# Attention with Sinkhorn-sorted blocks, then a four-expert MLP: expert 0's token weights loaded as six rows and turned on TensorE

## The chip, the cores and the metric

The kernel runs on one core of a Trainium2 chip. A core has five engines with a queue each: PE (TensorE, matmuls; its weight loads are listed as PEld), DVE (VectorE), ACT (ScalarE), POOL (GpSimd) and SP (SyncE, which here only issues DMAs). Data comes from HBM through 16 DMA engines into SBUF, which has 128 partitions; matmuls write to PSUM. The metric is the device time of one execution in microseconds (us).

## The reference

Batch 4, 8 heads, 768 tokens, head size 64. Sinkhorn normalization makes 8x8 mixing weights per head; they mix the eight blocks of 96 keys and values; each block of queries attends to its mixed block. The result, 3072 tokens of 512, goes through four experts of 512 x 1024 x 512, and the experts' outputs are added with a weight per token and expert.

```python
    for _ in range(5):
        P = P - np.max(P, axis=-1, keepdims=True)
        P = np.exp(P)
        P = P / (np.sum(P, axis=-1, keepdims=True) + 1e-09)
        P = P / (np.sum(P, axis=-2, keepdims=True) + 1e-09)
    k_sorted = np.einsum('bhij,bhjcd->bhicd', P, k_b).reshape(B, H, S, D)
    v_sorted = np.einsum('bhij,bhjcd->bhicd', P, v_b).reshape(B, H, S, D)
...
    p = domain_probs / (domain_probs.sum(-1, keepdims=True) + 1e-09)
    for e in range(E):
        h = np.maximum(x @ w1[e], 0.0)
        out += p[:, e:e + 1] * (h @ w2[e])
```

The change concerns `domain_probs`, 3072 x 4 float32 numbers, of which it touches the rows of the first batch, 768 x 4.

## The kernel before

The order of every engine's work is written out by hand: what stands first in the code comes first in its engine's queue. The stages are: the Sinkhorn steps on 32 partitions (one per batch and head); the attention of batch 0; then the experts for batch 0 while the attention of batch 1 runs between them, and so on, in chunks of 256 tokens; at the end the experts alone.

**The weights of the tokens** are wanted in two forms. For experts 1 to 3 (and for expert 0 later on) they are a row over tokens, copied to all partitions; `spread_weights` makes it through HBM. For expert 0 in batch 0 the second product is made whole for 128 tokens at a time, with the tokens on partitions, so the weight is one number per partition: `p_sb`, 128 x 6, six being the number `R` of token groups of 128 in a batch. `own_weights` computes it in four small DVE operations (L263 to L266) from `p_own`, which holds, on partition p, the four experts' numbers of tokens p, 128 + p, and so on. `second_layer0` uses it (L748) when it moves the product out of PSUM. `p_own` is loaded by SP at L171, with the third DMA of its queue: on the HBM side the pieces are four numbers, 16 bytes, 768 pieces in all. `p_own` lives in a corner of `Tt[2]`, which is unused until later; `room` is a 128 x 4 x 512 float32 tile that first gets the outputs of `second_layer0`.

**The start of each queue.** SP: L77 (the mixing weights), L170 (all of `domain_probs`, in long pieces), L171. POOL: the loads of the first half of the queries (two, L152) and of K (L113), the identity matrix `ident` (two instructions of `make_identity`), the loads of V, K, V (L113) and four of `w1sb[0]` (L183), then masks (L191 to L200), constants, its half of `sn16` (L330), two more loads of queries, two of `w2sb[0]` (L146), whose issue waits for earlier loads to land. PE: `warm(84)`, 84 matmuls on a constant whose result nobody reads; the transposes of the queries `h_q` (L288); `warm(30)`; `r_half(0)`, four matmuls that spread `sn16` over partitions (L342); `mix_half` for K and V, which begins with eight more matmuls on the constant (L507) and then mixes (L521); `r_half(1)`; the scores (L576); and so on. DVE: the Sinkhorn steps (L315 to L321), with the steps of `spread_weights` between them, its half of `sn16` (L330), then `build_PI0` (L353), which turns `ps_R`, the result of `r_half(0)`, into the mixing matrix that L521 reads.

**PSUM.** Two pools of two buffers each, `psM` and `psA`, every buffer of two banks. A tile of `psM` takes the buffer of the last but one tile before it and waits until that one's readers are through. The first tiles of `psM` are, in turn: `warm(84)`'s, `warm(30)`'s, `ps_R`, the first `mix_half`'s. Where the pools are closed for the last stage (`last_banks`, L1104), the tiles that follow lie over the old buffers.

Of the kernel before, what the change touches and what calls it, by code (L numbers as in the profile page):

```python
# [10 lines left out]
F32 = mybir.dt.float32  # L11
# [7 lines left out]
def kernel(  # L19
# [11 lines left out]
    nc = tc.nc  # L31

    B, H, S, D = q.shape
# [4 lines left out]
    E = moe_w1.shape[0]  # L38
    FF = moe_w1.shape[2]
    P = 128  # L40
# [3 lines left out]
    R = BLK // CP  # L44
# [27 lines left out]
    def psm(shape, dtype, name):  # L72
        return psM.tile(shape, dtype, tag="ps", name=name)
# [27 lines left out]
    room = const.tile([P, 4, Dm], F32, name="room")  # L101
# [5 lines left out]
    def load_natural(b, nm, qd, parts=1, between=None):  # L107
        src = {"k": k, "v": v}[nm]
        t = arena[:, ds(("k", "v").index(nm) * 2 * NW + qd * NW, NW)].rearrange("p (h r d) -> p h r d", h=4, r=R)
        natural[(b, nm, qd)] = t  # L110
        n = 4 // parts
        for m in range(0, 4, n):
            nc.gpsimd.dma_start(  # L113
                t[:, ds(m, n)].rearrange("p h r d -> p h (r d)"),
                src[b, ds(4 * qd + m, n)].rearrange("h (p r) d -> p h (r d)", r=R),
            )
            if m == 0 and between:
                between()
# [31 lines left out]
    def load_half_queries(hf):  # L150
        for qd in range(2):
            nc.gpsimd.dma_start(  # L152
                q0[ds(64 * qd, 64), hf].rearrange("p h r d -> p h (r d)"), half_queries(qd, hf)
            )
# [7 lines left out]
    def p_part(at, n):  # L162
        return Tt[2].rearrange("p a f x -> p (a f x)")[:, ds(2 * at, 2 * n)].bitcast(F32)
# [4 lines left out]
    p_own = p_part(2 * E * NT + NT, R * E).rearrange("p (t e) -> p t e", e=E)  # L168
    own_den = p_part(2 * E * NT + NT + R * E, R).rearrange("p (t o) -> p t o", o=1)
    nc.sync.dma_start(p_in, moe_domain_probs.rearrange("(p t) e -> p t e", t=NT))  # L170
    nc.sync.dma_start(p_own, moe_domain_probs[0:S].rearrange("(t p) e -> p t e", p=P))  # L171
    load_half_queries(0)
    load_natural(0, "k", 0)


    ident = const.tile([P, P], F16, name="ident")
    make_identity(nc, ident)
    load_natural(0, "v", 0)
    load_natural(0, "k", 1)
    load_natural(0, "v", 1)  # L180
# [91 lines left out]
    def warm(n):  # L272
        ps = psM.tile([P, 4, P], F32, tag="ps", name=f"ps_w_{state['n']}")
        state["n"] += 1
        for m in range(n):
            nc.tensor.matmul(ps[:, m % 4, :], dummy, dummy, start=True, stop=True)
# [3 lines left out]
    def h_q(qd, hf, copy, ps=None):  # L280

        if ps is None:
            ps = psa([P, 2, R, 64], F16, f"ps_q_{qd}_{hf}")
        rows = ds(64 * qd, 64)
        for sg in range(2):
            for r in range(R):
                for hh in range(2):
                    nc.tensor.transpose(  # L288
                        ps[ds(D * hh, D), sg, r, :], q0[rows, hf, 2 * sg + hh, r, :], ident[rows, rows]
                    )  # L290
        if copy:
            copy(qT0[qd][:, :, hf], ps[:])
# [16 lines left out]
    for it in range(5):  # L309
        nc.scalar.activation(sn[:], sn[:], AF.Exp, bias=0.0, scale=1.0)  # L310
        if it == 4:
            for qd in range(2):
                h_q(qd, 0, nc.scalar.copy)
            warm(30)
        nc.vector.tensor_reduce(srow[:], sn[:], AX.X, ALU.add)  # L315
        nc.vector.reciprocal(srow[:], srow[:])
        nc.vector.tensor_tensor(sn[:], sn[:], srow[:].broadcast_to([GH, NB, NB]), ALU.mult)
        nc.vector.tensor_reduce(scol[:], sn[:].rearrange("p i j -> p j i"), AX.X, ALU.add)
        nc.vector.reciprocal(scol[:], scol[:])
        if it < 4:  # L320
            nc.vector.tensor_tensor(  # L321
                sn[:], sn[:],
                scol[:].rearrange("p j o -> p o j").broadcast_to([GH, NB, NB]),
                ALU.mult,
            )
            if it:
                next(p_steps)

    for a, eng in enumerate((nc.vector, nc.gpsimd)):
# [4 lines left out]
            ALU.mult,  # L334
        )

    ps_R = psM.tile([P, 2, 512], F32, tag="ps", name="ps_R")
    Rv = ps_R[:, :, 0:HB * GH].rearrange("p a (i g) -> p a i g", g=GH)

# [1238 lines left out]
```

## Time and profile before

| | us |
|---|---|
| median of 3 runs | 358.63 |
| lowest, highest of them | 358.15, 358.74 |
| the profiled execution | 358.21 |
| its span, from the first to the last instruction | 356.3 |
| PE idle in 0 to 11.60, of 11.60 | 2.30 |
| PE idle in 11.60 to 20, of 8.40 | 0.60 |
| PE idle in 20 to 320, of 300 | 0.14 |
| PE idle in 320 to 356.3 | 2.86 |

Lines of the profile are read so: start and length in us, engine, line of the kernel, operation, what it writes and reads, the shapes, the count; in brackets the idle time of the engine before it, and who ended it. In the groups by line, the numbers behind the bar are busy time and mean ns of one. In tables by stretch, each engine's busy time is followed by the granted PE clock, the busy share of the DMA engines (over 1 where several packets of one engine are under way) and GB/s.

The loads of the first 60 us stand one behind another: the page has the DMA engines busy for at least nine tenths of nearly every slice up to 140 us, at some 200 GB/s.

```profile
DMA  8999999999999999743995410005200014100021
GB/s 104 203 205 230 212 209 194 207 195 167 195 180 166 195 116 203 138 88 44 180 205 91 107 74 0 2 1 136 78 26 3 2 37 141 62 0 2 0 75 46
```

### The profile page before, as it was taken

The numbers are of one execution on the slowest core, as the hardware profiler recorded it, in microseconds if no ns is written. First come the engines' busy times: TensorE is split into PE (matmuls) and PEld (weight loads), VectorE is DVE, ScalarE is ACT, GpSimd is POOL, SyncE is SP. The second block draws the span as 40 slices with busy tenths as digits, with TensorE's granted clock in tenths as the row PEclk, the third lists the DMA queues.
The fourth block names the chain that finished last, engine by engine and source line by source line (L and its number), as shares of the span: only waits on it lengthen the run. The fifth ranks groups of instructions, "written<-read, shape, count | busy, mean of one in ns | idle before, by whom it ended". The sixth has DMA issues, their size and how long they took to land.

```text
span 356.3 us, 9511 instructions
## 1 busy us (share of the span) xinstructions
PE 350.4 (98%) x3948; PEld 305.5 (86%) x3948; DVE 277.5 (78%) x555; ACT 170.1 (48%) x302; POOL 137.6 (39%) x154
## 2 busy tenths in 40 slices
PE   8899999999999999999999999999999999999996
PEld 8686857888888888988899888888888888888886
DVE  5766787779798687778879988896678886588963
ACT  2653330452425445368847259830288611598301
POOL 8766112466022420000626318840068800188400
PEclk9999999999999999999999999999999999999999
DMA  8999999999999999743995410005200014100021
GB/s 104 203 205 230 212 209 194 207 195 167 195 180 166 195 116 203 138 88 44 180 205 91 107 74 0 2 1 136 78 26 3 2 37 141 62 0 2 0 75 46
DMA packets 74762, 40.26 MB, mean 113 GB/s; under 512 B 41568, under 2 KB 70496, under 8 KB 74720
## 3 DMA queue, kind: packets, MB, share of 16 engines
q0 software_dynamic: 38720, 19.93, 43.2%
q1 hardware_dynamic: 35856, 19.67, 27.2%
q8 instruction: 31, 0.51, 0.6%
q14 instruction: 11, 0.09, 0.1%
q10 hardware_dynamic: 144, 0.07, 0.1%
HBM read 41.88 MB, written 6.34 MB: 135 GB/s over the span
## 4 chain that ended last, share of the span: by engine, by line
PE 95%; DVE 3%; issue 0%; DMA 0%; ACT 0%; DVEq 0%
PE ps_h L815 18%; PE ps_Q L1296 18%; PE ps_p L799 12%; PE ps_X L1153 10%; PE ps_Z L1153 7%; PE ps_Q L1153 7%; PE ps_Z L1296 6%; PE ps_h L704 3%; PE ps_o L741 3%; PE ps_p L860 3%; PE ps_a L479 2%; PE ps_s L444 2%; PE ps_k L425 1%; PE ps_v L391 1%; PE ps_mv L521 1%; PE ps_a L593 0%
## 5 line engine op out<-in xcount | busy, mean ns | idle before, releaser
L815 PE MATMUL ps_h<-xT,w 128*128 128x256 f16 x576 | 67.5, 273 | 0.0
L815 PEld LDWEIGHTS <-w 128*128 128x128 f16 x576 | 55.2, 98 | 7.3
L821 DVE SCALAR_TENSOR_TENSOR Hb<-ps_h,pb 128x1024 f16<-128x1024 f32 x34 | 41.5, 1223 | 17.8 <-PE ps_h L815 17.6
L1153 PEld LDWEIGHTS <-w 128*128 128x128 f16 x480 | 43.6, 98 | 4.7
L1166 POOL TENSOR_TENSOR arena<-tmp,pb 128x512 f16<-128x512 f32 x12 | 15.2, 1276 | 65.7 <-PE ps_Z L1153 49.8
L1296 PEld LDWEIGHTS <-Hb 128*128 128x128 f16 x320 | 31.1, 98 | 3.5
L1165 ACT ACTIVATE tmp<-tmp 128x512 f32<-128x512 f32 x46 | 29.0, 632 | 3.9 <-DVE tmp L1203 3.9
L1296 PEld LDWEIGHTS <-Sb 128*128 128x128 f16 x304 | 28.2, 98 | 3.0
L1153 PEld LDWEIGHTS <-arena 128*128 128x128 f16 x312 | 27.7, 98 | 2.8
L451 ACT ACTIVATE ET<-ps_s 96x768 f16<-96x768 f32 x24 | 18.1, 802 | 25.2 <-PE ps_s L444 25.0
L434 ACT CAST kT<-ps_k 64x384 f16<-64x384 f32 x48 | 22.7, 473 | 13.3 <-PE ps_k L425 12.3
L126 POOL DMA_DIRECT2D arena<-in_q_dram x24 | 19.9, 842 | 20.8 <-DMA q_ring<-arena 17.7
L1153 PE MATMUL ps_X<-ET,arena 128*128 128x256 f16 x168 | 25.2, 272 | 0.0
L1296 PE MATMUL ps_Q<-w,Hb 128*128 128x256 f16 x192 | 24.6, 273 | 0.0
L799 PEld LDWEIGHTS <-Hb 128*128 128x128 f16 x232 | 21.9, 98 | 3.0
L1159 DVE SCALAR_TENSOR_TENSOR Hb<-ps_X,pb 128x512 f16<-128x512 f32 x27 | 18.7, 692 | 7.0 <-PE ps_X L1153 7.0
L1173 ACT COPY ps_X<-ps_Z 128x512 f32<-128x512 f32 x27 | 15.4, 571 | 17.8 <-PE ps_Z L1153 17.8
L1153 PE MATMUL ps_Z<-xT,w 128*128 128x256 f16 (+1 forms) x176 | 22.5, 258 | 0.0
L785 DVE TENSOR_TENSOR Sb<-Hb 128x512 f16<-128x512 f16 x33 | 20.6, 646 | 0.0
L1180 ACT COPY tmp<-ps_X 128x512 f32<-128x512 f32 x26 | 15.2, 586 | 9.2 <-PE ps_X L1153 6.6
L1159 DVE SCALAR_TENSOR_TENSOR Hb<-ps_Z,pb 128x512 f16<-128x512 f32 x27 | 18.4, 683 | 1.3 <-PE ps_Z L1153 1.3
L1203 DVE TENSOR_TENSOR tmp<-ps_Q,tmp 128x512 f32<-128x512 f32 x26 | 17.7, 683 | 0.8 <-PE ps_Q L1153 0.8
(270 smaller groups left out, 744.3 us busy)
## 6 DMA issues: line engine op xcount, KB each, us to landing
w<-in_moe_w_dram POOLq DMA_DIRECT2D x4, 1024.0 KB, 27.2
w<-in_moe_w_dram POOLq DMA_DIRECT2D x6, 512.0 KB, 19.7
arena<-in_k_dram POOLq DMA_DIRECT2D x7, 384.0 KB, 7.6
arena<-in_v_dram POOLq DMA_DIRECT2D x7, 384.0 KB, 8.1
vs<-arena SPq DMA_DIRECT2D x36, 66.0 KB, 5.3
arena<-in_q_dram POOLq DMA_DIRECT2D x24, 96.0 KB, 7.5
out_dram<-ob SPq DMA_DIRECT2D x9, 256.0 KB, 2.0
pb<-p_dram SPq DMA_DIRECT2D x4, 512.0 KB, 5.8
```

What stands on the lines that cost most here:

```text
L126: nc.gpsimd.dma_start(t[:, h // 2, :, h % 2, :], q[b, h].rearrange("(t p) d -> p t d", p=P))
L434: nc.scalar.copy(kT[ds(D * hh, D), r], pk[ds(D * r, D), hh].rearrange("p a (i c) -> p a i c", c=CP),)
L451: nc.scalar.activation(ETs[2 * (pr % 2) + hh][:, 0:S].rearrange("c (a x) -> c a x", a=2), pss[hh][0:BLK, :, 0:HS], AF.Exp, bias=0.0, scale ...
L785: tt(sm[0], blk(0, 1), blk(1, 1), ALU.add)
L799: nc.tensor.matmul(ps, lhs(e, f), Ts[e][rhs][:, f, :], start=(first and e == es[0] and f == 0), stop=(done and e == es[-1] and f == KH - 1 ...
L815: nc.tensor.matmul(ps[:, f, :], w1sb[e][:, kc, ds((4 * g + f) * P, P)], xT[:, kc, ds(2 * c * P, 2 * P)], start=(kc == 0), stop=(kc == NKC ...
L821: nc.vector.scalar_tensor_tensor(out=Hb[:, homes.get(e, e), ds(4 * g, 4), :], in0=ps[:], scalar=0.0, op0=ALU.max, in1=weights(e).broadcast ...
L1153: nc.tensor.matmul(dst[:, ds(f * cols, cols)], a[lhs][:, k, ds((f0 + f) * P, P)], t[rhs][:, k, :], start=(first and f == 0 and k == 0), st ...
L1159: nc.vector.scalar_tensor_tensor(out=home(i, j), in0=src.rearrange("p (f x) -> p f x", f=m), scalar=0.0, op0=ALU.max, in1=weight(j).broadc ...
L1165: nc.scalar.activation(src, src, AF.Relu, bias=0.0, scale=1.0)
L1203: tt(t12, Q, u2, ALU.add)
L1296: nc.tensor.matmul(ps, lhs(e, f), Ts[e][rhs][:, f, part], start=(first and e == 0 and f == 0), stop=(e == E - 1 and f == KH - 1), skip_gro ...
```

## The change

The load at L171 now fills six partitions of `room` instead of 128 of `p_own`: row t holds the 512 numbers of tokens 128 t to 128 t + 127, one piece of 2 KB. POOL copies the 6 x 6 corner of the identity as float32 into `room`, right behind `make_identity`. The second warming loop makes 14 matmuls instead of 30. Behind the Sinkhorn steps, between the two halves of `sn16` and `ps_R` in the code, PE multiplies, for each expert e, the six rows' numbers of that expert (128 weight columns, a step of four numbers) with the identity into `ps_own`, a new tile of `psM`; DVE copies the 24 numbers per partition to `p_own`, where `own_weights` reads them as before. Both operands are float32.

```diff
-    nc.sync.dma_start(p_own, moe_domain_probs[0:S].rearrange("(t p) e -> p t e", p=P))
+    own_rows = room[0:R, 1, :].rearrange("t (p e) -> t p e", e=E)
+    nc.sync.dma_start(own_rows, moe_domain_probs[0:S].rearrange("(t p) e -> t p e", p=P))
     load_half_queries(0)
     load_natural(0, "k", 0)
...
     ident = const.tile([P, P], F16, name="ident")
     make_identity(nc, ident)
+    ident32 = room[0:R, 0, 0:R]
+    nc.gpsimd.tensor_copy(ident32, ident[0:R, 0:R])
     load_natural(0, "v", 0)
...
             for qd in range(2):
                 h_q(qd, 0, nc.scalar.copy)
-            warm(30)
+            warm(14)
...
+    ps_own = psm([P, E, R], F32, "ps_own")
+    for e in range(E):
+        nc.tensor.matmul(ps_own[:, e, :], own_rows[:, :, e], ident32, start=True, stop=True)
+    nc.vector.tensor_copy(p_own.rearrange("p t e -> p e t"), ps_own[:])
     ps_R = psM.tile([P, 2, 512], F32, tag="ps", name="ps_R")
```

In the queues: PE has the four products behind the 14 warming matmuls and ahead of L342; DVE has the copy between L330 and L353; POOL has its copy ahead of the loads of V, K, V and of `w1sb[0]`; SP and ACT have the same instructions in the same order. In `psM`, `ps_own` follows `warm(14)`'s tile, `ps_R` takes that one's buffer, and the first `mix_half`'s tile takes the buffer of `ps_own`, so that L507 waits for DVE's copy where it waited for `warm(30)`. From there on every tile of `psM` lies in the other buffer than before.

## The prediction

> **What bounds the kernel now.** I read the page first: the busy times, the slices, the chain of work that ended last.
>
> ```profile
> span 356.3 us, 9511 instructions
> ...
> PE 350.4 (98%) x3948; PEld 305.5 (86%) x3948; DVE 277.5 (78%) x555; ACT 170.1 (48%) x302; POOL 137.6 (39%) x154
> ...
> PE   8899999999999999999999999999999999999996
> ...
> PE 95%; DVE 3%; issue 0%; DMA 0%; ACT 0%; DVEq 0%
> ```
>
> PE is busy for 350.4 of 356.3 us. The 5.9 us in which it isn't lie almost wholly in the first two slices and the last one. So from about 20 us on, whatever the start has lost or gained goes one to one into the end, and nothing that the change touches after that (the four small operations that make the weights, at 21 us on DVE) is on PE. The question is only what happens to the first 20 us. There I read the time lines of PE and DVE, in order of time.
>
> ```profile
> 7.73 0.85 PE L288 MATMUL ps_q<-ident,T 64*64 64x64 f16 x48
> 8.51 1.85 PE L276 MATMUL ps_w<-Hb 128*128 128x128 f16 x30
> 11.60 0.26 PE L342 MATMUL ps_R<-ident,sn 32*128 32x32 f16 x4 [1.24 <-DVE sn L330]
> 11.79 0.62 PE L507 MATMUL ps_mk<-Hb 128*128 128x128 f16 x8
> ```
>
> ```profile
> 10.86 0.68 DVE L330 TENSOR_TENSOR sn<-sn,scol 32x512 f16<-32x512 f32 x1
> 11.97 0.75 DVE L353 TENSOR_TENSOR Sb<-maskk,ps_R 128x256 f16<-128x256 f16 x2 [0.43 <-PE ps_R L342]
> ```
>
> Up to 11.54 us DVE runs the Sinkhorn steps without a break, and PE only fills time: 30 warming matmuls to 10.36 us, then 1.24 us of idling until DVE's L330 releases L342. DVE then idles 0.43 us until L342 is through. The change puts its PE work into the first of these gaps and its DVE copy into the second.
>
> The third place is the loads. The weight-load rows of PE around 16 us, and the issue of the last V load (issued at 5.62 us):
>
> ```profile
> 15.86 0.20 PEld L576 LDWEIGHTS <-kT 64*128 64x128 f16 x8
> 16.14 0.46 PEld L521 LDWEIGHTS <-arena 128*64 128x64 f16 x24
> ...
> ```
>
> ```profile
> arena<-in_v_dram POOLq DMA_DIRECT2D x1, 384.0 KB, 10.5
> ```
>
> L576's weight loads end at 16.06, L521's begin at 16.14, and the V rows that they read land at 5.62 + 10.5 = 16.1. So here PE waited for a DMA, for some 0.08 us; it is too short for the list of waits. All other early loads have room: the K rows before them (issued 4.88, 9.3 us to landing: 14.2) are used at 14.40, the last part of w1 (issued 8.43, 13.0 us: 21.4) at 21.84.
>
> **The change, part by part.** The sum is made against the profiled execution: 358.21 us, of which the span is 356.3. The median of the runs is 358.63, 0.42 more.
>
> *Sixteen warming matmuls go.* Thirty take 1.85 us, 0.056 each after the pipeline's 0.2, so 0.90 us less of PE: the fourteen are through issuing at 8.51 + 14 x 0.056 = 9.3 us instead of 10.2. They write nothing that is read: off the path. Their cover is the idle stretch; what they could cost by missing is the clock (second rival).
>
> *Four float32 matmuls come, at 9.3 us.* Their inputs are long there: the six rows are issued at 1.66, as the old load was (landed 3.9 us later), and POOL's copy of the identity is done before 5 us. No row is float32. Low end: L342, the same kind of small product (128 weight columns, 32 moving), four in 0.26 us. High end: the slowest weight load and the slowest matmul of L276 (151 and 314 ns), not overlapped and doubled for operands twice as wide: 4 x 0.93 = 3.7 us. Nearest is L342, so I take it doubled for the width, 0.5 us: end at 9.8. They must be done by 11.54, so up to 2.2 us (0.55 each) costs nothing; at the high end they end at 13.0, 1.4 us late.
>
> [...]
>
> *DVE's copy out of PSUM*, 24 values per partition: low 0.16 us, high 0.31 (DVE's L263 and L252 on float32 rows of 6 and 96 values); I take 0.20, the mean of L606, which reads float32 from PSUM. It starts behind L330 at 11.57 and ends at 11.77, at 11.88 at the high end: both before 11.97, when L353 starts, which waits for L342 anyway. Queued behind it on DVE is L353, and PE's L521 waits for that. Cost 0.
>
> *PSUM ring.* The new tile is one more in a ring of two, so the warming matmuls of L507 now wait for DVE's copy. Copy end plus the 0.06 us that L342 took after L330 is 11.83, against 11.79 before: 0.04 us later (0.15 at the high end). But L521 starts at 12.45, 0.06 behind the first half of L353 (11.97 + 0.75/2 = 12.35 or a little later), and eight matmuls at 0.056 from 11.83 are issued by 12.28. Cost 0. All later tiles of the ring swap places, with the same predecessors in time.
>
> *POOL's copy of 6x6* stands ahead of three K and V loads, four w1 loads, the masks and POOL's half of L330. Low 0.13 us (POOL's L210), high 0.37 (L191, 128x64); I take 0.2. The loads: each is issued more than 7 us before it lands, behind a backlog, below. POOL's L330 ends at 12.46 + 0.2, or 12.83; PE's second L342, which waits for it, starts at 13.32. Cost 0; without that cover it would be the 0.2.
>
> *The load.* The DMA view of 2.70 to 5.05 us, by queue (packets, MB, share of 16 engines):
>
> ```profile
> q0 software_dynamic: 346, 0.25, 73.5%
> q1 hardware_dynamic: 784, 0.01, 26.9%
> ```
>
> The 768 pieces of 16 bytes are in q1: 26.9% of 2.35 us is 0.63 us of every engine. Six packets of 2 KB take their place. What follows in the backlog (q, k, v, w1 in turn; the rows below are two stretches of it, with DMA share and GB/s last) can land up to 0.63 us sooner; from below, 0 if the engines weren't the limit. Either way PE gains at 16.14 only what it waited, 0 to 0.08 us, since from 16.06 on it is held by its own order and by DVE. I take half, 0.04, but in a run that lies above the profiled one more of it may be this wait.
>
> ```profile
> 2.75:3.75 1.00, 1.00 (x12) 1.00 (x11) 0.86 (x5) 0.00 (x0) 0.98 (x2) 1.00 0.38 30
> 3.75:5.00 1.25, 1.25 (x15) 1.25 (x13) 0.82 (x5) 0.26 (x1) 1.19 (x3) 1.00 1.54 183
> ```
>
> Sum: 0 + 0 + 0 + 0 + 0 - 0.04: 358.17 against 358.21; for the median of runs about 358.5.
>
> **The rivals.**
>
> *Float32 matmuls too long (slower).* Place: PE between 9.3 and 11.54; it decides from 0.55 us for each on. Then L342, L353 and all behind them shift. For it: nothing in the trace shows their price, and the high end of the rows is beyond the point. Against: the small products here pipeline at 65 ns each. Price 0 to 1.4 us; with a typical 1.2: 359.8.
>
> *The clock of PE falls (slower).* From 1.06 to 5.04 us the time line has 38 matmuls in 3.98 us, from 5.04 to 7.60 it has 49 in 2.56: the same matmul, at half the rate first. If the thinner stretch from 9.3 to 11.6 brought that state back for another 4 us, PE, busy for 3.71 of the 4.00 us from 11.60, would lose up to half of that: 1.85 us, 360.5. Against: the 1.24 us of idling did not do it, and with the new matmuls at 0.5 us the idling is 1.8 us.
>
> *The loads gain more (faster).* The first row above moves 30 GB/s while the 16-byte pieces are at their thickest, the second 183. If the pieces cause that, 1.00 x (1 - 30/183) = 0.84 us come on top of the 0.63. What PE can take of it is the wait at 16.14 in an ordinary run: 0.08 and, if all that lies between the median and the profiled execution is this wait, 0.42 more, and a little behind it where w1's parts follow closely; 0.5 to 0.9 us, 357.9. Against: the second row runs at the full rate with the pieces still in it, and the other waits have room.
>
> *It doesn't do what it says.* The second row speaks for it: nothing lands sooner, and nothing is lost: 358.6.
>
> **How the numbers follow.** Forecast 0.42 (358.5, own range 358.1 to 358.9); no effect on the loads 0.24; long matmuls 0.13; the clock 0.07; loads gain more 0.14. 0.2% is 0.7 us, about what a measurement of this kernel can tell from no change. Of the last case I count two thirds beyond it (0.09), and 0.03 of the first two for scatter: faster 0.12. Of the long matmuls three quarters (0.10), the clock wholly (0.07) and 0.03 of scatter: slower 0.20. Same: 0.68. The range reaches down to 357.8, through most of the faster case, and up to 359.8, the typical long matmul; it leaves out the clock and the tails, under 0.2.
>
> **What would show it.** In the profile after: fourteen L276 rows and then four products on the new tile that end before 11.54; the DVE copy between L330 and L353, L353 still at 11.97; L507 about 0.04 later, L521's first start the same; POOL's half of L330 0.2 us later; V's last landing before 16.06 and the 0.08 us of PE's loads gone; PE's 40.00 of 40.00 later on unchanged. I am wrong if L342 starts after 11.60, if the matmuls behind it take twice their time, or if the end differs by more than what has been gained or lost at 20 us.

## The result, and the profile after

The changed kernel takes 359.9 us (median of 11 runs, 358.86 to 362.4) against 358.43 before on the same chip (11 runs, 358.04 to 359.75): 1.0039 times the time before, 95% interval 1.002 to 1.0058. It is slower, by 1.5 us in the medians. The profiled execution takes 360.24 us, its span is 358.3, 2.0 longer than before.

The page of the changed kernel: busy times, PE's row of slices, the granted clock, the chain that ended last.

```profile
span 358.3 us, 9499 instructions
...
PE 354.0 (99%) x3940; PEld 309.3 (86%) x3940; DVE 277.7 (78%) x556; ACT 170.5 (48%) x302; POOL 137.8 (38%) x155
...
PE   8999999999999999999999999999999999999996
...
PEclk9789999999999999999999999999999999999999
...
PE 99%; DVE 0%; issue 0%
```

PE is busy for 3.6 us more than before, although 16 warming matmuls of 0.056 us are gone. What is new is in the row of the granted clock, the 7 and 8 of the second and third slices; before, this row is 9 throughout:

```profile
PEclk9999999999999999999999999999999999999999
```

Cut into stretches (us, busy time and count of PE, PEld, DVE, ACT and POOL, granted clock, DMA share, GB/s), the changed kernel has:

```profile
7.10:13.93 6.83, 6.65 (x156) 6.28 (x155) 4.95 (x20) 1.97 (x5) 6.58 (x21) 1.00 1.27 190
13.93:20.76 6.83, 6.83 (x129) 5.77 (x124) 3.64 (x8) 4.94 (x9) 4.52 (x6) 0.50 1.26 204
20.76:60.00 39.24, 39.10 (x515) 28.49 (x513) 29.79 (x54) 14.49 (x20) 14.19 (x19) 1.00 1.28 211
```

From 13.93 to 20.76 us PE's clock is granted at half, and in no other stretch behind 7.10 us. Before, the clock is 1.00 from 5.04 us to the last matmuls. The two ends lie 6.83 us apart, twice the 3.41 us for which the clock is at half in one of the kernels below (v1, from 12.54 to 15.95). All 11 timed runs of the changed kernel have a mean clock of 0.986 to 0.995; of 117 runs of the kernel before, over all the comparisons below, three do.

The time lines of PE and of DVE after, in the form of those shown of before:

```profile
8.71 0.85 PE L291 MATMUL ps_q<-ident,T 64*64 64x64 f16 x48
9.49 0.96 PE L279 MATMUL ps_w<-Hb 128*128 128x128 f16 x14
10.38 2.02 PE L342 MATMUL ps_own<-room 6*128 6x6 f32 x8
12.27 0.25 PE L349 MATMUL ps_R<-ident,sn 32*128 32x32 f16 x4
12.70 0.61 PE L514 MATMUL ps_mk<-Hb 128*128 128x128 f16 x8 [0.18 <-DVE T L343]
```

```profile
11.06 0.68 DVE L333 TENSOR_TENSOR sn<-sn,scol 32x512 f16<-32x512 f32 x1
...
12.44 0.20 DVE L343 COPY T<-ps_own 128x24 f32<-128x24 f32 x1 [0.70 <-PE ps_own L342]
12.63 0.75 DVE L360 TENSOR_TENSOR Sb<-maskk,ps_R 128x256 f16<-128x256 f16 x2
```

The four products are eight matmuls, each with a weight load, and take 2.02 us. DVE waits 0.70 us for them, and L360 (L353 before) starts at 12.63 instead of 11.97. The copy L343 is now what L514 waits for.

The loads did land earlier: the K and V rows of the first halves are issued at 2.71, 4.30, 5.06 and 5.80 us and land at about 9.5, 11.5, 13.7 and 15.4 (issue plus 6.8, 7.2, 8.6 and 9.6 us), the last one 0.7 us earlier than the 16.1 of before. (With the six rows alone, y2 below, that row lands at 16.4, so the gain isn't even sure to be theirs.) At half the clock PE comes to them later anyway.

### The profile page after: what moved, and what is told of

Its sections match the earlier page's. It is cut to its first block, busy times and chain, and to the rows that moved or that the text cites. A ratio compares the mean times of both kernels' runs of the same rounds, so it can differ in the third digit from the quotient of the medians.

```text
span 358.3 us, 9499 instructions
## 1 busy us (share of the span) xinstructions
PE 354.0 (99%) x3940; PEld 309.3 (86%) x3940; DVE 277.7 (78%) x556; ACT 170.5 (48%) x302; POOL 137.8 (38%) x155
## 4 chain that ended last, share of the span: by engine, by line
PE 99%; DVE 0%; issue 0%
PE ps_h L822 18%; PE ps_Q L1303 18%; PE ps_p L806 12%; PE ps_X L1160 10%; PE ps_Z L1160 7%; PE ps_Q L1160 7%; PE ps_Z L1303 6%; PE ps_o L748 3%; PE ps_h L711 3%; PE ps_p L867 3%; PE ps_w L279 2%; PE ps_a L486 2%; PE ps_s L451 2%; PE ps_k L432 1%; PE ps_v L398 1%; PE ps_s L583 1%
## 5 line engine op out<-in xcount | busy, mean ns | idle before, releaser
L1303 PEld LDWEIGHTS <-Sb 128*128 128x128 f16 x304 | 28.2, 98 | 3.0
L1180 ACT COPY ps_X<-ps_Z 128x512 f32<-128x512 f32 x27 | 15.4, 571 | 17.7 <-PE ps_Z L1160 17.7
```

What stands on the lines that cost most here:

```text
L1303: nc.tensor.matmul(ps, lhs(e, f), Ts[e][rhs][:, f, part], start=(first and e == 0 and f == 0), stop=(e == E - 1 and f == KH - 1), skip_gro ...
```

## The experiments

Times are medians; the ratio is to the kernel before on the same chip, whose medians there are 358.32 to 358.37 us (358.43 beside the changed kernel). It is an estimate from all runs and need not be the quotient of the medians. "Clock low" counts the runs whose mean granted clock is below 0.998. Line numbers shift by a few from kernel to kernel.

| kernel | first, second warming | products | us (range) | ratio, 95% interval | clock low |
|---|---|---|---|---|---|
| after | 84, 14 | float32 | 359.9 (358.86 to 362.4) | 1.0039 (1.002 to 1.0058) | 11 of 11 |
| x1 | 84, 30 | float32 | 359.33 (358.82 to 361.71) | 1.0048 (1.0027 to 1.0069) | 2 of 7 |
| x2 | 84, 14 | none | 359.75 (359.0 to 360.41) | 1.0039 (1.0027 to 1.0051) | 5 of 5 |
| x3 | 84, 30 | none | 358.97 (358.1 to 361.67) | 1.0033 (1.0013 to 1.0053) | 2 of 12 |
| x4 | 84, 30 | float16 | 360.0 (358.11 to 361.8) | 1.0038 (1.002 to 1.0055) | 5 of 12 |
| y1 | 84, 30 | none | 358.1 (357.88 to 360.1) | 1.0002 (0.9989 to 1.0016) | 1 of 12 |
| y2 | 84, 30 | none | 358.41 (358.07 to 359.31) | 0.9995 (0.9985 to 1.0006) | 0 of 12 |
| y3 | 84, 14 | none | 360.42 (358.83 to 362.5) | 1.005 (1.0033 to 1.0067) | 12 of 12 |
| y4 | 84, 44 | none | 360.13 (359.85 to 360.6) | 1.0047 (1.0033 to 1.0061) | 0 of 5 |
| z1 | 76, 30 | float32 | 359.58 (358.05 to 361.42) | 1.0026 (1.0008 to 1.0044) | 7 of 12 |
| z2 | 68, 30 | none | 359.71 (358.12 to 360.99) | 1.0024 (1.0008 to 1.0041) | 11 of 12 |
| z3 | 84, 22 | none | 358.04 (358.02 to 358.67) | 0.9992 (0.9981 to 1.0004) | 0 of 11 |
| z4 | 92, 30 | none | 359.16 (358.37 to 360.69) | 1.0027 (1.001 to 1.0043) | 0 of 12 |
| v1 | 84, 14 + 16 thin | none | 359.8 (358.61 to 361.27) | 1.0033 (1.0018 to 1.0048) | 11 of 12 |
| v2 | 84, 15 wide | none | 358.23 (358.04 to 359.01) | 0.9992 (0.9981 to 1.0003) | 0 of 12 |
| v3 | 84, 15 wide | float32 | 358.71 (358.13 to 360.37) | 1.0007 (0.9992 to 1.0023) | 1 of 12 |

**First four: warming against products.** All are the changed kernel with an edit.

x1, the warming matmuls back:

```diff
-            warm(14)
+            warm(30)
```

> The changed kernel with the second warming loop at 30 matmuls again; the float32 products stay behind it. Three theories of the 1.5 us. Clock: PE's rate is halved for one or more stretches of 3.4 us, because the float32 products (8 records, 0.23 us apart, six columns each) keep PE occupied and let almost nothing pass; then the products still lie in front of L342 and the rate falls in most runs, mean clock 0.995 or below, and 359 to 361 us. Late: the products end too late, and 16 warming matmuls more push them 0.9 us further back: clock 1.000 and 0.5 to 0.9 us over the changed kernel's undisturbed time, 359.0 to 359.5. Warming: the 16 missing matmuls alone starved the clock: clock 1.000 in all runs.

x2, no products (a constant stands where they wrote), 14 warming matmuls; x3, the same with `warm(30)`:

```diff
-    ps_own = psm([P, E, R], F32, "ps_own")
-    for e in range(E):
-        nc.tensor.matmul(ps_own[:, e, :], own_rows[:, :, e], ident32, start=True, stop=True)
-    nc.vector.tensor_copy(p_own.rearrange("p t e -> p e t"), ps_own[:])
+    nc.vector.memset(p_own, 0.25)
```

> The four products and the copy out of PSUM are left out, a constant is written to p_own instead (expert 0's weights in batch 0 are wrong numbers); six-row load, POOL's copy and warm(14) stay. Clock by what PE streams: without the products the stretch is just as thin, so the rate still falls, mean clock 0.990 to 0.995, 359 to 360. Products themselves (their lateness, or a clock that only they disturb): clock 1.000, 358.2 to 358.5.

> As the one without products, with 30 warming matmuls: what is left of the change is the load of six rows and POOL's 6x6 copy. All theories: clock 1.000, and the time of the kernel before less what the earlier loads bring, 0 to 0.5 us: 358.0 to 358.4. Slower than 358.8 would mean that the load or POOL's copy has a price.

x4, the rows cast to float16 on POOL, the products in float16, and `warm(30)`:

```diff
+    own16 = room[0:R, 0, 0:2 * P].bitcast(F16).rearrange("t (e p) -> t e p", e=E)
+    nc.gpsimd.tensor_copy(own16, own_rows.rearrange("t p e -> t e p"))
...
+        nc.tensor.matmul(ps_own[:, e, :], own16[:, e, :], ident[0:R, 0:R], start=True, stop=True)
```

> The products in float16 (POOL casts the six rows, 6x512, in place of its 6x6 copy; the weights are rounded to float16), 30 warming matmuls. If the float32 form is what costs, four records of under 0.1 us each stand in place of 1.9 us of products: clock 1.000 and 358.1 to 358.5. If four more products and a copy cost in any form: 358.8 or more.

Without the products but with 14 warming matmuls the clock fell in every run and the time stayed at that of the changed kernel: the products are not what the loss hangs on. With 30 the clock held in five of seven runs (x1) and ten of twelve (x3), yet the medians did not come back wholly: 359.33 and 358.97. In float16 the products take four matmuls in 0.25 us, half of what the prediction took for float32:

```profile
9.68 0.25 PE L342 MATMUL ps_own<-ident,room 6*128 6x6 f16 x4
```

That kernel's seven runs with the clock held lie between 358.11 and 360.3, and in five of twelve it fell. It also changes more than the type: POOL's cast of the rows takes 1.14 us where the 6x6 copy took 0.18, and the first V load behind it is issued at 5.14 us instead of 4.30. This group told the clock from the products, but left x1, x3 and x4 unexplained: two runs of x3 stand at 361.18 and 361.67, one of x1 at 360.75 and two of x4 at 360.03 and 360.3, at a clock of 0.999 or 1.0. No profile of such a run was taken, and nothing later settled them.

**Second four: each part alone.** y1, y2 and y3 are the kernel before with one part of the change. y1, POOL's copy only:

```diff
+    ident32 = room[0:R, 0, 0:R]
+    nc.gpsimd.tensor_copy(ident32, ident[0:R, 0:R])
```

> The kernel before with one addition: POOL's 6x6 float32 copy behind the identity. With it (changed kernel and three variants) DVE's first L321 took 0.28 to 0.34 us in place of 0.21, and the Sinkhorn steps ended 0.14 to 0.2 us later. Theory POOL: that copy alone moves L330 from 10.86 to 11.0 us, so 0.14 us in an undisturbed run (358.4 to 358.6), and PE, idle longer, loses its clock in some of the runs (359 to 361.7), as in the variant without products and with 30 warming matmuls. Theory load: the six-row load disturbs, POOL's copy does not: 358.0 to 358.7 as before, no run above 359.

y2, the six-row load only (with the constant of x2 for `p_own`):

```diff
-    nc.sync.dma_start(p_own, moe_domain_probs[0:S].rearrange("(t p) e -> p t e", p=P))
+    own_rows = room[0:R, 1, :].rearrange("t (p e) -> t p e", e=E)
+    nc.sync.dma_start(own_rows, moe_domain_probs[0:S].rearrange("(t p) e -> t p e", p=P))
...
+    nc.vector.memset(p_own, 0.25)
```

> The kernel before with the six-row load alone (no 6x6 copy on POOL, no products, 30 warming matmuls; p_own gets a constant, so expert 0's weights in batch 0 are wrong numbers). Theory POOL: nothing is prolonged, V's last rows land at 15.4 to 15.8 us instead of 16.1: 358.0 to 358.4, no run above 359. Theory load: spread as in the variant with POOL's copy, median near 359, some runs at 361.

y3, 14 warming matmuls only:

```diff
-            warm(30)
+            warm(14)
```

> The kernel before with 14 warming matmuls in place of 30 and nothing else. Theory clock by what PE streams: PE is thin from 9.3 to 11.6 us whatever else is there: the rate falls in all or most runs, mean clock 0.995 or lower, 359 to 360.4 us. If the 16 matmuls don't matter for the clock and only the products or POOL's copy do: 358.0 to 358.7, clock 1.000.

y4, x3 with `warm(44)` in place of `warm(30)`:

> Six-row load and POOL's copy, no products (a constant in p_own), and 44 warming matmuls: PE streams to about 11 us, with 14 x 0.056 = 0.8 us less idling. Theory clock: no run loses the rate, 358.2 to 358.6, the 0.14 us of POOL's copy remaining; in an execution whose rate rises late they end behind the Sinkhorn steps and cost up to 0.5 us. If the slow runs of the variant with 30 have another cause (loads, DVE), they stay: some at 360 to 361.7.

POOL's copy alone (y1) and the load alone (y2) do nothing that can be measured. Both together, as x3 has them, gave 1.0033 on another chip; that difference stays open. Taking the sixteen warming matmuls from the kernel before, and nothing else, gives the whole loss, and the lower clock in 12 of 12 runs. Its stretches:

```profile
6.50:13.30 6.80, 5.13 (x150) 4.71 (x150) 5.19 (x21) 1.91 (x5) 6.58 (x20) 1.00 1.24 178
13.40:20.10 6.70, 6.70 (x124) 5.64 (x119) 3.64 (x8) 4.80 (x9) 4.04 (x6) 0.50 1.26 205
```

The same half clock, with nothing new on PE. The runs fall into steps by their mean clock: two at 0.995, 358.83 and 358.84; those at 0.99 from 359.64 to 359.78; at 0.986 from 360.36 to 360.72 (one more, 362.5 at 0.99, fits no step). One step lower costs 0.8 to 0.9 us; as an estimate, 0.004 to 0.005 of a span of some 358 us is 2.9 to 3.6 us more at half rate. How many steps it is differs between executions of this one kernel.

y4 is listed at a clock of 1.0 in every run and still takes 360.13. (Its profile and x1's hold no clock rows, so the listed 1.0 is no proof by itself; but its matmuls run at the full rate: the 24 of L525 at 14.59 us take 0.57 us, as in the kernel before, against 0.85 in the changed kernel at half the clock.) Its list of waits in 18 to 33 us (engine, what waited, for what: total, times, longest) holds two stops that no shown event ends:

```profile
PE ps_a L597 <- issue: 0.8, 1, 0.8
PE ps_w L552 <- issue: 0.8, 1, 0.8
```

So a second way of losing time came up, with more instructions on PE, not fewer. z4 was made for it.

**Third four: where, how many, and the count.** z1 is the changed kernel with `warm(76)` and `warm(30)`; the other three are the kernel before with `warm(68)` (z2) or `warm(92)` (z4) in the first group, or `warm(22)` in the second (z3).

```diff
-    warm(84)
+    warm(68)
```

> The changed kernel with the 30 warming matmuls ahead of the float32 products and the first warming cut from 84 to 76, so that PE issues as many instructions ahead of L349 as in the kernel before (a float32 product takes two weight loads and two matmuls, four products as much as eight warming matmuls). Theory (the 16 matmuls that are missing right ahead of the products cost the clock; the float32 products themselves only delay the start by up to 0.5 us, most of which is taken up by 68 us; the 1.0 us of the run with 30 and 84 was mostly a stall of PE that moved with the count of instructions): every run at a granted clock of 1.0, 358.3 to 358.9 us. Rival (the products themselves cost the microsecond, wherever PE's instructions fall): 359.2 to 359.5 again. Rival (the products' 2 us of thin work lower the clock also here): a clock of 0.99 in most runs, 359.7 to 360.4.

> The kernel before with the first warming cut from 84 to 68 and nothing else: 16 warming matmuls fewer, as in the run with 14 instead of 30, but taken from the first group, and the same count of PE's instructions as there. Theory (it is the work right ahead of L342 that keeps the clock): all or nearly all runs at 1.0 and 358.1 to 358.6 us. Rival (it is the number of warming matmuls, or of instructions, wherever they stand): a clock of 0.995 to 0.986 and 359.6 to 360.6 us as in that run.

> The kernel before with 22 instead of 30 warming matmuls in the second group. Theory (a bound that is passed or not: with 30 the clock held in nearly every run, with 14 in none): runs of two kinds, at a clock of 1.0 and about 358.2 us, and at 0.99 and 359.7 to 360.0 us. Rival (each missing warming matmul costs its share): all runs near 359.3 us at a clock between.

> The kernel before with the first warming raised from 84 to 92 and nothing else: 16 instructions of PE more ahead of L342 (a load and a matmul each), as many as the changed kernel with 30 warming matmuls has; nothing on the critical path, and the clock kept. Theory (a stall of PE that waits for nothing the profile shows moves with the count of instructions): clock 1.0 and 358.8 to 359.3 us, with an issue wait of 0.7 to 1 us in PE's rows somewhere behind 18 us. Rival (the count does nothing, and the microsecond in the run with 30 and 84 came from the products): 358.1 to 358.5 us.

Three of these theories fell. Taking the sixteen from the first group lowers the clock as well (z2, 11 of 12 runs): it is not the place right ahead of L342 that counts. With 22 all eleven runs kept it (z3): neither two kinds of runs nor a share for each missing matmul, but a bound between 14 and 22. And in z1, with the 30 right ahead of the products but eight fewer in the first group, the clock fell in 7 of 12, though the profiled run kept it; its five runs that kept it stand at 358.05 to 359.29, median 358.41 against 358.35 before. z4's theory came true: with eight warming matmuls more, off the path, it lost 0.8 us in the medians at a full clock in all runs. Its profile, of its quickest run (358.37), has a shorter stop of the same kind, and one of 0.2 us at L704:

```profile
13.63 0.29 PE L521 MATMUL ps_mv<-Sb,arena 128*64 128x64 f16 x7 [0.39 <-issue]
```

That more instructions on PE can cost time is shown by z4's median, 359.16 against 358.35. What PE waits for in these stops no view of this case shows, and no run tests it.

The profiles now allowed a table. Cut from the rise of its clock into stretches of 3.41 us, half of the 6.83 above, each execution has one stretch ahead of the kernel's end in which PE does the least while the clock is full. Its work is counted as rows x weight columns x streamed columns of the matmuls that start in it, in units of a warming matmul (128 x 128 x 128; at 0.056 us 61 of them fill a stretch; by L741 of before, where 24 matmuls of 512 columns take 5.18 us, 63, of which 20.5 and 21.6 are 0.32 and 0.34).

| execution | stretch from | matmuls | work | clock after it |
|---|---|---|---|---|
| z2 | 8.19 | 17 | 17.0 | 0.5 |
| after | 10.51 | 63 | 19.3 | 0.5 |
| y3 | 9.95 | 58 | 20.5 | 0.5 |
| x2 | 10.28 | 64 | 20.5 | 0.5 |
| x4 | 10.57 | 64 | 20.5 | 0.5 |
| z4 | 12.95 | 66 | 21.6 | 1.0 |
| z3 | 8.82 | 27 | 23.2 | 1.0 |
| y1 | 10.57 | 72 | 23.3 | 1.0 |
| z1 | 8.28 | 32 | 24.0 | 1.0 |

The work orders them; the number of matmuls doesn't (64 and a fall, 27 and none), nor does busy time (PE is busy for 95% of that stretch in the changed kernel, 50% in z3). Idle time doesn't either; the same row in y3's stretch and in z3's, with the idle time at its end:

```profile
L342 PE MATMUL ps_R<-ident,sn 32*128 32x32 f16 x4 | 0.3, 174 | 1.6 <-DVE sn L330 1.6
L342 PE MATMUL ps_R<-ident,sn 32*128 32x32 f16 x4 | 0.3, 174 | 1.7 <-DVE sn L330 1.7
```

y3 idles for 1.6 us and loses the clock, z3 for 1.7 and keeps it. Of the other profiles with clock rows, before, x3 and y2 do least with 30 to 32 and keep it. That was a fit to profiles already seen, so it had to foretell something.

**Last three: is it the work?** v1 and v2 are the kernel before, v3 the changed kernel; `warm` gets a second loop: v1 has 14 matmuls as they were and 16 `thin` ones, v2 and v3 have 15 `wide` ones and none of the old.

```diff
+        for m in range(thin):
+            nc.tensor.matmul(ps[:, m % 4, :], dummy[0:8], dummy[0:8], start=True, stop=True)
...
+        for m in range(wide):
+            nc.tensor.matmul(
+                ps[:, ds(2 * (m % 2), 2), :], dummy,
+                dummy.rearrange("p (o x) -> p o x", o=1).broadcast_to([P, 2, P]), start=True, stop=True,
+            )
```

> The kernel before with 14 warming matmuls of 128 rows and then 16 of 8 rows in place of 30 of 128: as many instructions and as much busy time of PE as before, but of the work of the array (rows by columns by streamed columns) that of 14 and one more. Theory (the clock goes by the work of the array in a stretch of 3.4 us: in the profiles so far it fell behind stretches with at most 0.32 of the full work and held behind all with 0.34 and more): it falls in nearly all runs as with 14, to 0.995 to 0.986, 358.8 to 360.6 us with a median near 359.8. Rival (it goes by busy time or by the number of matmuls): a clock of 1.0 and 358.0 to 358.7 us as before.

> The kernel before with 15 warming matmuls of 256 streamed columns in place of 30 of 128 in the second group: the same work of the array in half the instructions. Theory (work of the array): a clock of 1.0 in nearly all runs, and 358.0 to 358.7 us. Rival (the number of matmuls): a lower clock and 359.6 to 360.6 us as with 14.

> The changed kernel with 15 warming matmuls of 256 streamed columns in place of its 14 of 128: the work of 30, with one instruction more than it has. Theory (the loss is the clock; the products are late by up to 0.5 us at 12 us and most of that is taken up by 68 us): a clock of 1.0 in most runs, and those at 358.1 to 358.9 us. Rival (the float32 products cost a part to the end): runs at a clock of 1.0 at 358.9 to 359.4 us. Rival (the products' 2 us with little work lower the clock in spite of it): a clock of 0.995 to 0.99 in most runs.

All three came out as the work has it. The groups of PE in the thinnest stretch of v1 and then of v2 (shapes of weights and of the moving operand, count, busy time, mean ns; the counts include matmuls that began just before it):

```profile
L278 PE MATMUL ps_w<-Hb 8*128 8x128 f16 x16 | 1.1, 215 | 0.0
L276 PE MATMUL ps_w<-Hb 128*128 128x128 f16 x12 | 0.8, 219 | 0.0
L509 PE MATMUL ps_mk<-Hb 128*128 128x128 f16 x8 | 0.6, 221 | 0.0
...
L344 PE MATMUL ps_R<-ident,sn 32*128 32x32 f16 x4 | 0.3, 174 | 0.8 <-DVE sn L332 0.8
```

```profile
L278 PE MATMUL ps_w<-Hb 128*128 128x256 f16 x13 | 1.6, 272 | 0.0
L512 PE MATMUL ps_mk<-Hb 128*128 128x128 f16 x8 | 0.6, 221 | 0.0
L347 PE MATMUL ps_R<-ident,sn 32*128 32x32 f16 x4 | 0.3, 175 | 1.3 <-DVE sn L335 1.3
```

In v1 a matmul on 8 rows takes as long as one on 128 (215 and 219 ns), and it idles 0.8 us where v2 idles 1.3. Yet v1's clock falls (work 19.5, 11 of 12 runs) and v2's holds (28.2, 12 of 12), with half the instructions. v3 gives the changed kernel its work back and can't be told from no change. No version here beats the kernel before: v2 and z3, both at 0.9992, can't be told from it either. What the products still cost is seen there without the clock:

```profile
10.26 2.03 PE L347 MATMUL ps_own<-room 6*128 6x6 f32 x8
12.15 0.25 PE L354 MATMUL ps_R<-ident,sn 32*128 32x32 f16 x4
```

```profile
12.33 0.20 DVE L348 COPY T<-ps_own 128x24 f32<-128x24 f32 x1 [0.60 <-PE ps_own L347]
12.52 0.75 DVE L365 TENSOR_TENSOR Sb<-maskk,ps_R 128x256 f16<-128x256 f16 x2
```

The build of the mixing matrix is 0.55 us late, and the span is 356.7 against 356.3 before and v2's 356.3; in the medians v3 lies 0.48 above v2, with intervals that overlap.

## Why the prediction was wrong

It said 358.5, with 359.8 as the upper end, and no change that can be told; the time is 359.9.

**The step that failed** is the first term, the sixteen matmuls: "off the path. Their cover is the idle stretch; what they could cost by missing is the clock (second rival)". It was put at 0; alone it costs 2.05 us in the medians (y3, 360.42 against 358.37). The rival was then put aside with "the 1.24 us of idling did not do it, and with the new matmuls at 0.5 us the idling is 1.8 us", and given 0.07. That weighed the wrong quantity, idle time, and took a state that holds for proof of a margin. The margin was there, but small: the thinnest stretch with 22 warming matmuls held, with 14 it fell every time (z3, y3). The new products were counted there as time in which PE isn't idle; they fill time but hardly any of the array: by their shape, 6 rows and 6 streamed columns, all four are less than 0.02 of one warming matmul.

The half rate lasted 6.83 us in the changed kernel and 3.41 in v1. It came after a stretch with 1.6 us of idle time (y3) and, in the changed kernel, after one in which PE was busy for 3.24 of 3.42 us, while z3 idled for 1.7 us and kept the clock. How long PE may idle without losing the clock no run shows.

**The rival's size** was 1.85 us, from 4.0 us at half rate. It lasted 6.83 us, yet y3's span is only 1.4 us longer than before, not 3.2 (half of the 6.44 us that PE was busy between 13.5 and 20.5). PE idled for 0.56 of those 7 us before and for none in y3, and the rows shown take 1.4 to 1.5 times as long, not twice; before, then y3:

```profile
13.59 0.35 PE L576 MATMUL ps_s<-Sb,kT 64*128 64x96 f16 x8
14.40 0.57 PE L521 MATMUL ps_mk<-Sb,arena 128*64 128x64 f16 x24
```

```profile
13.85 0.50 PE L576 MATMUL ps_s<-Sb,kT 64*128 64x96 f16 x8
14.95 0.85 PE L521 MATMUL ps_mk<-Sb,arena 128*64 128x64 f16 x24
```

**The products** were mis-sized: 0.5 us taken, 2.02 measured, within the range of 0.26 to 3.7. The row that was nearest by shape was the wrong one: the trace shows two weight loads and two matmuls for each float32 product, of 324 and 371 ns each at the median, against one of each, of 91 and 171 ns, for L342 of before. By the break-even of 2.2 us even 2.02 would have fitted, if PE had come to them at 9.3; in the profiled execution the clock rose at 7.10 us instead of 5.04, the first 84 warming matmuls ended a microsecond later, and the products began at 10.38. So the first rival came true too, in small: 0.4 us of the span in v3.

**What the rest did.** L360 did not stay at 11.97, because of the products, and the PSUM ring's wait (L514 for DVE's copy, 0.18 us) became real with it. POOL's copy took 0.18 us and cost nothing (y1), as foreseen. The load's gain at 16 us can't be seen: y2, with the six rows alone, is at 0.9995, with an interval that leaves at most 0.5 us, so the third rival's 0.5 to 0.9 is all but out. DVE's copy took 0.20 us as said. That what is lost at 20 us comes out whole at the end held: y3's profile and the changed kernel's are 1.8 and 2.4 us late at 20 us by the starts of ACT's instructions, and 1.4 and 2.0 in the span; the difference of 0.4 is the profiled execution of before, which lost as much between 20 and 68 us where that of z3 (span 356.1) did not.

In sum, of the 2.0 us in the span about 1.4 is the clock (y3) and the rest, 0.6, goes with the products (0.4 in v3, where they came 0.12 us sooner). This split rests on one profile each: against z3's, the clock's part is 1.6 of 2.2, and over all runs y3 is no quicker than the changed kernel (1.005 and 1.0039, with intervals that overlap).

## What to carry to other kernels

Matmuls that nobody reads may be the cheapest work in a kernel: here sixteen of them take 0.89 us off the path (30 in 1.85, 14 in 0.96), and without them the kernel took 2.05 us more (y3). Before some are cut, count the array work (rows x weight columns x streamed columns) around them, not the idle time or the number of instructions; in the profiles here the clock fell where the thinnest stretch of 3.41 us at full clock had at most 20.5 warming matmuls' work, and held where it had 21.6 or more. Keep well clear of the thinnest stretch that is known to hold. If instructions must be saved, fewer and wider matmuls may do (15 of 256 columns for 30 of 128 kept the clock in 12 of 12 runs, v2). And measure what a float32 matmul takes: four products of 6 x 128 by 6 x 6 took 2.02 us here, with less work than 0.02 of one warming matmul.

## What the runs showed of the hardware

- The granted clock went from 1.0 to 0.5 for 6.83 us in the profile of the changed kernel and for 3.41 us in v1's, and back. How much of an execution it was at half differs between executions of one kernel and, with that, the time: the mean clock of y3's runs is 0.995, 0.99 or 0.986, all but one of them from 358.83 to 360.72 us. All falls seen in profiles followed a stretch with at most 20.5 warming matmuls' work, no stretch with 21.6 or more was followed by one. The bound rests on one profile for each kernel (without x1 and y4, which hold no clock rows), and was not tried more closely. What brings the clock back was not tested: it took 3.41 us in v1, 6.83 in the others.
- A float32 product of 6 x 128 by 6 x 6 is two weight loads and two matmuls, 2.02 us for four (the changed kernel); the float16 form of the same four took 0.25 us (x4).
- More instructions on PE, off the path and at a full clock, cost 0.8 us in the medians (z4); y4, with 14 more matmuls in the second group, stands 1.8 us above the kernel before. Both show stops of PE of 0.2 to 0.8 us that nothing in the list of waits ends. What PE waits for in them no run tests, and how much of x1's and x3's time is of this kind stays open.
